# Where GpSimd scales the low words of a weight chunk within a period: behind the masks, or ahead of the clamp

## The chip, the cores and the metric

One core of one Trainium2 chip. The time is that of the device for one execution, in microseconds (us), as the median over several runs. The profile and the trace are of one execution each. The engines are TensorE (PE in the profile; PEld is its weight loads), VectorE (DVE), ScalarE (ACT), GpSimd (POOL) and SyncE (SP), which here issues DMAs.

## What is computed

Attention with a threshold, and behind it a feed-forward block with a squared ReLU:

```python
scores = scale * np.matmul(q, k.transpose(0, 1, 3, 2))      # 8 x 8 heads, 576 x 576, head_dim 64
thresh = np.max(scores, axis=-1, keepdims=True) - tau
scores = np.where(scores >= thresh, scores, -1000000000.0)
attn = np.exp(scores - np.max(scores, axis=-1, keepdims=True))
attn = attn / (np.sum(attn, axis=-1, keepdims=True) + 1e-09)
x = np.matmul(attn, v)                                       # -> 4608 x 512
h = np.maximum(x @ w_in, 0.0)                                # w_in 512 x 2048
return (h * h @ w_out).astype(np.float32)                    # w_out 2048 x 512
```

q, k and v are float32. The two weights are float64: the kernel receives them as 64-bit words and makes float32 of them itself, with integer operations on the two 32-bit halves (the low word and the high word of each number).

## The kernel before

**Stages.** The attention runs first, to about 500 us of the span. Then come the hidden layer and the output layer, both as matrix products with fewer multiplications (seven products of sub-blocks in place of eight, used twice), whose sums and differences VectorE and GpSimd make. The weights are converted from float64 while the attention runs, and are used after it.

**Periods.** The attention works on units of 128 rows of two heads. A period p handles units A = 2p and B = 2p+1. The order in which a period's instructions are issued is written out by hand as a list of step names; each step issues its instructions to its engine, and every engine works through its own in that order. There are two lists: PLAIN, and CONVERTING for the periods in which a chunk of a weight is converted. There are 32 chunks, chunk m starting in period m+2, so that the CONVERTING list is used in periods 2 to 34 (`starts` and `converts`).

**The steps of a period that matter here.** On VectorE: `topA0` to `topB1` (L452) read the scores out of PSUM and take the row maxima; `inv` (L477) takes the reciprocal of the sums of the previous period's units; `maskA1` to `maskB1` (L467) apply the threshold and sum the rows. On ScalarE: `powA0` to `powB1` (L462) are the exponentials, and `eU`, `eV`, `eW`, `x` move results out of PSUM. On GpSimd: `leastA` and `leastB` (L459) make the thresholds from the maxima; `over` (L474) adds 1e-9 to the previous period's sums, which `inv` reads; `xm` (L669) multiplies the previous outcome by the reciprocals. On PE: `SA`, `SB` (L434) are the scores, `U`, `V`, `W` (L380, and L515 for the reciprocals) transpose the weights of the attention, `PV` (L532) multiplies them with the values, `T` (L398) turns later queries and keys.

**The conversion of a chunk** of 128 x 512 numbers goes through six steps over two periods. `fetch` (L191) loads it two periods ahead. In its own period p: `c1` (L205, ScalarE) takes the absolute value of the high words, `c2` (L212, GpSimd) scales the low words in place, `c3` (L219, GpSimd) clamps what c1 made. In the next period: `c4` (L227, VectorE) shifts it, `c5` (L235, VectorE) merges it into the high words, `c6` (L245, GpSimd) adds the low words. So `c2` needs the loaded chunk alone, and only `c6`, a period later, needs what it makes:

```python
nc.gpsimd.tensor_scalar(out=lo, in0=lo.bitcast(U32), scalar1=2.0**-29, scalar2=None, op0=ALU.mult)   # c2, L212
...
nc.gpsimd.tensor_tensor(out=a, in0=hi, in1=lo, op=ALU.add)                                           # c6, L245
```

In CONVERTING periods GpSimd's own order is thus: c3, leastA, over, leastB, c2, c6 (of the chunk before), xm; VectorE's is topA0, topA1, topB0, topB1, c4, inv, maskA1, maskA0, maskB0, c5, maskB1.

Of the kernel before, what the change touches and what calls it, by code (L numbers as in the profile page):

```python
# [48 lines left out]
def kernel(  # L49
# [438 lines left out]
    for g in range(2, 2 * len(pairs)):  # L488
        two, x = divmod(g - 4, 4)
# [99 lines left out]
    def begun(n):  # L589
# [5 lines left out]
        maskB1  # L595
    """.split()
    CONVERTING = """
        fetch SA U eU T SB topA0 s1 c1 topA1 topB0 c3 V PV leastA over powA0 topB1
        powA1 powB0 c4 eT inv x maskA1 maskA0 W leastB maskB0 c5 eV c2 powB1 c6 eW maskB1 xm
    """.split()  # L600

    BEGIN_WITH = {
# [740 lines left out]
```

## Time and profile before

| what | value |
|---|---|
| median of 3 runs | 1300.32 us (1298.04 to 1300.54) |
| span of the profiled execution | 1298.2 us |
| PE busy | 1276.4 us (98%) |
| VectorE busy | 1007.0 us (78%) |
| ScalarE busy | 845.5 us (65%) |
| GpSimd busy | 926.8 us (71%) |
| L212 on GpSimd | 32 times, 65.1 us, first at 26.7 us, last at 246.9 us |
| L245 on GpSimd | 32 times, 47.4 us |
| L219 on GpSimd | 32 times, 19.6 us |
| L459, L474, L669 on GpSimd | 65.9, 17.0, 23.9 us |

The profile gives for each instruction its start, its duration and, where its engine stood idle before it, how long and what ended the wait. The shares are averages over three very different stages; what happens to the conversion is read from the stretch that holds L212, and in it from the order of the instructions in time. Matmuls are pipelined and their ends are modelled, so that PE's share says little of how near it is to its peak.

### The profile page before, as it was taken

What the parts mean: (1) busy time and instruction counts of PE and PEld (TensorE: products, weight loads), DVE (VectorE), ACT (ScalarE), POOL (GpSimd) and SP (SyncE); (2) the same over time, 40 slices, a digit from 0 to 9 for tenths busy, and PEclk for the clock granted to TensorE, in tenths of its full rate; (3) what the DMA queues carried; (4) which work ended last, traced back from release to release, by engine and by line L of the source; (5) the groups of instructions that cost most, each with busy time, mean ns of one, the idle gap of its engine ahead of it and who ended that gap; (6) DMA issues with size and microseconds to landing.
All of it is one profiled execution on the core that took longest, in us unless ns stands there. A gap on an engine that the chain in (4) does not pass through costs nothing.

```text
span 1298.2 us, 45819 instructions
## 1 busy us (share of the span) xinstructions
PE 1276.4 (98%) x18287; PEld 1117.7 (86%) x18287; DVE 1007.0 (78%) x2423; ACT 845.5 (65%) x1498; POOL 926.8 (71%) x1031
## 2 busy tenths in 40 slices
PE   8999999999999999999999999999999999999998
PEld 5777777677777778988888888999999999999998
DVE  6999999999999996886887878867646654665463
ACT  6999999888998984666765856675523432343240
POOL 2787878755555321888897989858787767777775
PEclk8999999999999999999999999999999999999999
DMA  5665566544333312667768768589554224522411
GB/s 143 163 160 154 153 192 180 149 103 110 85 79 80 92 34 64 191 183 218 212 186 226 218 175 235 162 304 391 195 159 164 83 86 159 163 80 88 160 34 34
DMA packets 291413, 196.20 MB, mean 151 GB/s; under 512 B 100096, under 2 KB 252160, under 8 KB 291200
## 3 DMA queue, kind: packets, MB, share of 16 engines
q1 hardware_dynamic: 289888, 192.87, 51.5%
q8 instruction: 144, 2.36, 0.8%
q14 instruction: 69, 0.57, 0.2%
q10 hardware_dynamic: 1312, 0.41, 0.1%
HBM read 120.85 MB, written 72.35 MB: 149 GB/s over the span
## 4 chain that ended last, share of the span: by engine, by line
PE 86%; ACT 5%; DVE 4%; DMA 3%; issue 2%; POOL 0%; SPq 0%; ACTq 0%; DVEq 0%; POOLq 0%
PE po L1077 28%; PE ph L935 16%; PE sc L532 11%; PE sc L434 10%; PE ph L942 10%; PE pt L380 6%; DVE arena L452 2%; PE sc L515 2%; PE sc L398 2%; ACT arena L462 1%; ACT arena L523 1%; DMA g<-arena 1%; PE sc L380 1%; DVE arena L125 1%; DMA wall<-w 1%
## 5 line engine op out<-in xcount | busy, mean ns | idle before, releaser
L125 POOL TENSOR_TENSOR arena<-arena 128x512 f32<-128x512 f32 (+1 forms) x314 | 378.1, 1222 | 147.0 <-DVE arena L125 119.3
L1077 PE MATMUL po<-wall,arena 128*128 128x128 f32 x3528 | 395.0, 275 | 1.9 <-ACT arena L752 1.4
L1077 PEld LDWEIGHTS po<-wall,arena 128*128 128x128 f32 x3528 | 394.4, 192 | 2.5 <-ACT arena L752 1.8
L125 DVE TENSOR_TENSOR arena<-ph,arena 128x512 f32<-128x512 f32 x378 | 255.1, 689 | 79.9 <-PE ph L935 31.5
L122 POOL TENSOR_TENSOR arena<-arena 128x128 f32<-128x128 f32 (+1 forms) x322 | 265.4, 825 | 23.0 <-DMA arena<-w 6.6
L935 PE MATMUL ph<-arena,wall 128*128 128x256 f32 x1176 | 256.6, 380 | 1.8 <-DVE arena L125 1.4
L935 PEld LDWEIGHTS ph<-arena,wall 128*128 128x128 f32 x1176 | 222.2, 190 | 35.9 <-DVE arena L125 5.4
L125 DVE TENSOR_TENSOR arena<-po,arena 128x128 f32<-128x128 f32 x378 | 108.2, 290 | 167.7 <-PE po L1077 163.4
L467 DVE SCALAR_TENSOR_TENSOR arena<-arena 128x576 f32<-128x576 f32 x288 | 235.7, 855 | 0.9 <-ACT arena L462 0.9
L791 ACT COPY c<-arena 128x512 f32<-128x512 f32 (+1 forms) x295 | 169.0, 578 | 71.8 <-DVE arena L122 35.8
L452 DVE TENSOR_SCALAR_CACHE_REDUCE arena<-sc 128x576 f32<-128x576 f32 x288 | 205.1, 748 | 10.9 <-ACT arena L523 4.3
L462 ACT ACTIVATE arena<-arena 128x576 f32<-128x576 f32 x288 | 208.7, 773 | 7.4 <-DVE arena L452 4.2
L532 PEld LDWEIGHTS sc<-arena 64*64 64x64 f32 x5760 | 159.2, 133 | 36.5 <-DVE arena L452 19.8
L532 PE MATMUL sc<-arena 64*64 64x128 f32 (+1 forms) x5760 | 180.5, 262 | 2.9 <-DVE arena L452 1.3
L434 PE MATMUL sc<-arena 64*64 64x64 f32 (+1 forms) x2304 | 176.2, 415 | 3.8 <-ACT arena L403 2.4
L523 ACT COPY arena<-pt 128x1024 f32<-128x1024 f32 x144 | 146.4, 1016 | 27.9 <-PE pt L380 26.5
L122 DVE TENSOR_TENSOR arena<-arena,c 128x512 f32<-128x512 f32 x235 | 154.4, 666 | 11.0 <-ACT c L791 7.6
L752 ACT COPY arena<-po 128x128 f32<-128x128 f32 x63 | 16.6, 264 | 186.4 <-PE po L1077 183.7
L942 PE MATMUL ph<-arena,wall 128*128 128x128 f32 x1176 | 132.0, 275 | 0.7 <-DVE arena L659 0.7
L942 PEld LDWEIGHTS ph<-arena,wall 128*128 128x128 f32 x1176 | 131.6, 192 | 1.1 <-issue 0.8
L380 PEld LDWEIGHTS pt<-ident,arena 64*128 64x128 f32 x2304 | 83.5, 139 | 40.0 <-ACT arena L523 30.1
L434 PEld LDWEIGHTS sc<-arena 64*64 64x64 f32 x2304 | 74.0, 134 | 42.2 <-issue 14.1
(54 smaller groups left out, 1079.7 us busy)
## 6 DMA issues: line engine op xcount, KB each, us to landing
arena<-g SPq DMA_DIRECT2D x144, 256.0 KB, 4.4
g<-arena SPq DMA_DIRECT2D x192, 128.0 KB, 2.9
w<-arena SPq DMA_DIRECT2D x60, 256.0 KB, 2.8
wall<-w SPq DMA_DIRECT2D x49, 256.0 KB, 5.2
g<-arena SPq DMA_DIRECT2D x48, 256.0 KB, 3.8
arena<-w SPq DMA_DIRECT2D x44, 256.0 KB, 3.3
arena<-in_v_dram SPq DMA_DIRECT2D x32, 288.0 KB, 3.8
out_dram<-arena SPq DMA_DIRECT2D x70, 128.0 KB, 2.2
```

What stands on the lines that cost most here:

```text
L122: e.tensor_tensor(out=out, in0=x, in1=y, op=ALU.subtract)
L125: e.tensor_tensor(out=out, in0=x, in1=y, op=ALU.add)
L380: made = nc.tensor.transpose(pt[:, r, ts(slot, HALF)], of[rows, :], ident[rows, rows])
L434: made = nc.tensor.matmul(sc[at, ds(to, count)], lhs, kT[rows, ds(at_k, count)], start=True, stop=True)
L452: made = nc.vector.tensor_scalar(out=s[:, j, :], in0=sc[:, ds(at, S)], scalar1=1.0, scalar2=None, op0=ALU.mult, op1=ALU.min, accum_out=nmx ...
L462: nc.scalar.activation(out=w[:, :, j, :], in_=of(j), func=AF.Exp, bias=nmx[:, j : j + 1], scale=-1.0)
L467: nc.vector.scalar_tensor_tensor(out=w[:, :, j, :], in0=of(j), scalar=thr[:, j : j + 1], in1=w[:, :, j, :], op0=ALU.is_le, op1=ALU.mult, a ...
L532: made = nc.tensor.matmul(sc[ds(u * D, D), ds(5 * j * BANK + row, count)], loaded_v[i][rows, (c - (u != j)) % CH, :], wT[m][rows, ds(weigh ...
L791: nc.scalar.copy(c, y)
L935: nc.tensor.matmul(to[:, 2 * j : 2 * j + 2, :], W_IN[m, k][:, ts(2 * h + j, P)], part_x(steps, k, m), start=(not more and j == 0), stop=Tr ...
L942: nc.tensor.matmul(to[:, j, :], W_IN[m, k][:, ts(j, P)], x, start=(not more and j == 0), stop=True, skip_group_check=True,)
L1077: nc.tensor.matmul(to, g[:, j, :], w[:, j, :], start=(not more and j == 0), stop=(j == 3), skip_group_check=True)
```

## The change

One name moves within one list. The step `c2` stands ahead of `c3`, and no longer behind `eV`:

```diff
     CONVERTING = """
-        fetch SA U eU T SB topA0 s1 c1 topA1 topB0 c3 V PV leastA over powA0 topB1
-        powA1 powB0 c4 eT inv x maskA1 maskA0 W leastB maskB0 c5 eV c2 powB1 c6 eW maskB1 xm
+        fetch SA U eU T SB topA0 s1 c1 topA1 topB0 c2 c3 V PV leastA over powA0 topB1
+        powA1 powB0 c4 eT inv x maskA1 maskA0 W leastB maskB0 c5 eV powB1 c6 eW maskB1 xm
     """.split()
```

GpSimd's order in these periods becomes c2, c3, leastA, over, leastB, c6 (of the chunk before), xm. The order on the other engines and of the DMAs stays as it was, and so do all instructions themselves. The list for the other periods is not touched.

## The prediction

> **What bounds the kernel now.** First the busy time of the engines by stretch, to see which engine is full where the diff acts. The scaling of the low words (L212) is found 32 times, from 26.7 to 246.9 us of the span, so the stretch to look at is about 33 to 255 us. Columns: length, then busy us of PE, PEld, DVE, ACT, POOL, then granted clock, DMA share, GB/s.
>
> ```profile
> core 0: us, PE busy (x) PEld busy (x) DVE busy (x) ACT busy (x) POOL busy (x), PEclk, DMA share, GB/s
> 100.00:140.00 40.00, 39.38 (x961) 29.17 (x958) 40.00 (x111) 38.55 (x70) 32.57 (x42) 1.00 0.59 152
> 33.00:255.00 222.00, 217.95 (x5390) 163.51 (x5386) 221.39 (x594) 213.55 (x385) 177.23 (x217) 1.00 0.62 165
> ```
>
> VectorE is busy without a gap; GpSimd has 18% left over. The page's 98% for PE is no bound here, since ends of matmuls are modelled. The timeline of one period, VectorE and GpSimd alone, shows why. Columns: start, duration, engine, line.
>
> ```profile
> 110.33 0.23 POOL L474 TENSOR_SCALAR arena<-arena 128x4 f32<-128x4 f32 x1
> 110.81 0.17 DVE L477 RECIPROCAL arena<-arena 128x4 f32<-128x4 f32 x1
> 110.89 0.79 DVE L467 SCALAR_TENSOR_TENSOR arena<-arena 128x576 f32<-128x576 f32 x1
> 111.13 2.05 POOL L212 TENSOR_SCALAR arena<-arena 128x512 int32<-128x512 uint32 x1
> 111.61 1.23 DVE L467 SCALAR_TENSOR_TENSOR arena<-arena 128x576 f32<-128x576 f32 x1
> ...
> 112.77 0.81 DVE L467 SCALAR_TENSOR_TENSOR arena<-arena 128x576 f32<-128x576 f32 x1
> 113.50 0.69 DVE L235 SCALAR_TENSOR_TENSOR arena<-arena 128x512 int32<-128x512 int32 x1
> 114.11 0.81 DVE L467 SCALAR_TENSOR_TENSOR arena<-arena 128x576 f32<-128x576 f32 x1
> 114.34 1.48 POOL L245 TENSOR_TENSOR wall<-arena 128x512 int32<-128x512 int32 x1 [1.17 <-DVE arena L235]
> ...
> 115.78 0.73 POOL L669 TENSOR_TENSOR arena<-arena 128x256 f32<-128x256 f32 x1
> 116.47 0.61 POOL L219 TENSOR_SCALAR arena<-arena 128x512 f32<-128x512 f32 x1
> 117.07 0.30 POOL L459 TENSOR_SCALAR arena<-arena,tau_p 128x2 f32<-128x2 f32 x1
> 117.42 0.23 POOL L474 TENSOR_SCALAR arena<-arena 128x4 f32<-128x4 f32 x1
> 117.56 0.42 DVE L227 TENSOR_SCALAR arena<-arena 128x512 int32<-128x512 int32 x1
> 117.89 0.17 DVE L477 RECIPROCAL arena<-arena 128x4 f32<-128x4 f32 x1
> ```
>
> Three things are to be seen. The period, reciprocal to reciprocal, is 117.89 - 110.81 = 7.08 us. GpSimd idles 1.17 us, but behind the scaling, waiting for the merge L235. And two engines form a ring: "over" (L474) must end before the reciprocal (L477), which heads VectorE's masks (L467) and the merge; the merge releases GpSimd's add (L245), then come the normalisation (L669), the clamp (L219), a threshold (L459) and the next "over". Now the ring nearly closes: over ends at 117.65, the reciprocal starts at 117.89. One period shows what happens when the clamp comes late (its operand was late by 1.01 us):
>
> ```profile
> 230.96 0.62 POOL L219 TENSOR_SCALAR arena<-arena 128x512 f32<-128x512 f32 x1 [1.01 <-ACT arena L205]
> 231.02 0.84 DVE L227 TENSOR_SCALAR arena<-arena 128x512 int32<-128x512 int32 x1
> ...
> 232.08 0.23 POOL L474 TENSOR_SCALAR arena<-arena 128x4 f32<-128x4 f32 x1
> 232.34 0.18 DVE L477 RECIPROCAL arena<-arena 128x4 f32<-128x4 f32 x1 [0.49 <-POOL arena L474]
> ```
>
> VectorE stood still for 0.49 us, and the reciprocal started 0.03 us after over ended (232.31). So the spare time of this ring is 117.89 - 117.65 - 0.03 = 0.21 us a period.
>
> **The change, part by part.** Nothing is added or removed: 32 scalings change their place in GpSimd's order, from behind leastB to ahead of the clamp of the same period. No DMA and no other engine's instruction moves. The moved instruction waits only for the load of its chunk, which is issued two periods earlier (14 us, against a median of 4.8 us to landing), so it brings no new wait of its own. What it is moved past are the clamp, leastA, over and leastB: all four now queue behind it, and behind over stand the reciprocal, the four masks and the merge on VectorE.
>
> What goes: the scaling ran beside the masks, and one mask each period took 1.23 us where its neighbours take 0.81; start to start 111.61 to 112.77 is 1.16 against 0.73, so 0.43 us. In its new place the scaling lies beside L452, which reads PSUM; the clamp lies beside L452 now at its plain 0.61 us, so I take the stretch to vanish. Were VectorE still the bound, its period would be 7.08 - 0.43 = 6.65 us.
>
> What comes: the ring, start to start from the rows above. Over's end to reciprocal 0.03; to the first mask 0.08; masks 0.72, 0.73 (without the stretch), 0.73; merge to add 0.84; add 1.44; normalisation 0.69; then the scaling, D, with 0.08 before the next instruction (26.70 + 1.97 to the following L669 at 28.75); clamp 0.60; leastA 0.35; over 0.23. Sum: 6.44 + 0.08 + D = 6.52 + D. The same sum for the kernel before, with the stretch and without the scaling, is 6.87, 0.21 under 7.08 as seen. The 1.17 us of idle time does not help: it stands ahead of the add, and the scaling is now behind it.
>
> D is the open price, since every scaling so far ran beside masks. It starts 0.48 us ahead of the end of one mask (111.61). A small L459 beside a mask shows what such a start means: it took 0.90 us from 232.41 and ended at 233.31, 0.16 us after the next mask began at 233.15, where it takes 0.29 alone; so about 0.13 us of it runs before it is held. The scaling ran 2.05 - 0.48 = 1.57 us past 111.61, and with 0.13 ahead of that D = 1.70. Bounds: 2.13 if it was never held (the longest of its 32), 0.61 as the row furthest away (the clamp, same shape). I take 1.70, by its own row. The ring is then 6.52 + 1.70 = 8.22 us, which is above 6.65, so GpSimd's part of the ring decides and VectorE idles 8.22 - 6.65 = 1.6 us ahead of each reciprocal.
>
> A rule of the Trainium skill bears on the stretch. Page "SBUF — State Buffer", section "Who interferes with whom": a VectorE instruction with two SBUF inputs contends with a GpSimd instruction that reads SBUF, and the later one is blocked until the first is done. The trace agrees on which rows suffer (masks yes, L452 no) and differs on how long: the mask lost 0.43 us of the scaling's 2.05. By the rule in full the shift L227 would now be caught beside the scaling; that outcome is a rival below.
>
> The sum over the stretch. From the reciprocal of the second period with a scaling (33.08) to that of the last (246.54) are 30 rings, 213.46 us now (30 x 7.08 and 1 us of small delays). The second period's own over ends at 32.27, and its scaling falls into 1.59 us in which GpSimd waited for L205 anyway (the first one into 5.17 us), so the new count starts at 32.30: 32.30 + 30 x 8.22 = 278.9 us. That is 32.4 later than 246.54. The period after the last scaling runs without the stretch, -0.4. Together +32.0 us. What follows (plain periods, then the two layers) has no catching up: it is a chain that starts later. The profiled execution has a span of 1298.2 us, 2.1 under the median of the runs, 1300.3; I carry the difference to the median: 1300.3 + 32.0 = 1332 us. With D = 1.57 (nothing of it runs before it is held) the ring is 8.09 and the sum +28; with D = 2.13 it is 8.65 and +45. So 1328 to 1345 for this case.
>
> ScalarE and PE should not add to that. PE goes from one recip fill (L380 at 111.37) to the next (118.62) in 7.25 us, under 8.22; ScalarE's Abs (L205), which the clamp needs, ends 1.5 us after the merge (115.68 against 114.19), some 4.5 us after over's end, and the clamp starts 7.0 us after it in the new ring.
>
> **The rivals.**
> - Slower still, by a collision: L227 (start 117.56) falls beside the scaling or the clamp, as at 231.02, where it took 0.84 instead of 0.42, and this time the clamp is the one that is held. Costs up to L227's 0.34 a ring: 8.56, 32.30 + 256.8 - 246.54 - 0.4 = +42, 1342 us. For it: L227 would start some 6.3 us after over's end, the scaling some 5.3. Against it: the one row shows L227 held, not GpSimd, and VectorE has time to wait. The rule quoted above gives this case.
> - Slower, but less, because the scaling is shorter undisturbed: with 1.28 us, the float add of the same shape (L125), the ring is 7.80 and the sum +19, 1320 us. Against it: 1.57 us of the scaling lie behind the mask that held it.
> - No change: D as short as the clamp, 0.61, gives a ring of 7.13 and 32.30 + 213.9 - 246.54 - 0.4 = -0.7, 1300 us. The point from which the ring decides is D = 0.55.
> - Faster: the scaling's cover holds, over is in time, and only the stretch goes: 32 x 0.43 = 13.8 us, 1287 us. This needs 6.52 + D under 6.65, D under 0.13, or an over that does not gate the reciprocal; the 0.49 us at 232 us speaks against the latter. The same for a change that does nothing: GpSimd's order does move, all 32 times.
>
> **How the numbers follow.** Forecast 0.75 (1328 to 1345), collision 0.10, shorter scaling 0.08, no change 0.03, faster 0.04. A measurement of this kernel can tell about 0.2% (2.6 us) from nothing; by these cases faster is 0.04, the same 0.03, slower 0.93. The range takes in the forecast's bounds, the collision and part of the shorter scaling: 1321 to 1347. The time is the forecast's, 1332.
>
> **What would show it.** Right: between 40 and 280 us a period of about 8.2 us; the wait of L477 for L474 about 30 times, 1.2 to 1.6 us each; L212 between L669 and L219 with about 1.7 us; no mask above 0.85 us; POOL L245 still waiting for L235, 2 to 2.7 us; last scaling near 275 us and everything after it later by one constant. Wrong: VectorE still gapless there with a period near 6.65 (over is no gate), L212 far under 1.5 us (D), L227 or L219 stretched (collision), or a wait of L477 that is made up for after 280 us.

## The result, and the profile after

The changed kernel takes 1335.35 us (1333.61 to 1335.68, 4 runs) against 1299.18 us (1297.27 to 1300.54, 4 runs) in the same comparison: 1.0278 times as long, 95% interval 1.0263 to 1.0293, or 36 us more. The profiled execution has a span of 1333.9 us, 35.7 more than the one before.

First the busy time by stretch, now to 285 us, since the last scaling has moved to 279.5 us (the columns are those of the same view before).

```profile
33.00:285.00 252.00, 214.13 (x5240) 149.09 (x5229) 220.09 (x575) 209.68 (x373) 175.56 (x210) 1.00 0.54 142
```

VectorE is busy for 220 us, as before (221), but now in 252 us and no longer in 222. What it waits for is in the view of its waits for this stretch (who waited, for whom, us in total, times, longest):

```profile
DVE arena L477 <- POOL arena L474: 31.9, 30, 1.1
```

30 waits of 1.06 us, all ahead of the reciprocal, all for "over". The timeline of one period, VectorE and GpSimd alone, shows what "over" is late for:

```profile
110.20 1.48 POOL L245 TENSOR_TENSOR wall<-arena 128x512 int32<-128x512 int32 x1 [2.17 <-DVE arena L235]
...
111.64 0.72 POOL L669 TENSOR_TENSOR arena<-arena 128x256 f32<-128x256 f32 x1
112.45 1.63 POOL L212 TENSOR_SCALAR arena<-arena 128x512 int32<-128x512 uint32 x1
113.42 0.94 DVE L227 TENSOR_SCALAR arena<-arena 128x512 int32<-128x512 int32 x1
114.16 0.66 POOL L219 TENSOR_SCALAR arena<-arena 128x512 f32<-128x512 f32 x1
114.80 0.29 POOL L459 TENSOR_SCALAR arena<-arena,tau_p 128x2 f32<-128x2 f32 x1
115.16 0.23 POOL L474 TENSOR_SCALAR arena<-arena 128x4 f32<-128x4 f32 x1
115.42 0.18 DVE L477 RECIPROCAL arena<-arena 128x4 f32<-128x4 f32 x1 [1.06 <-POOL arena L474]
...
116.23 0.81 DVE L467 SCALAR_TENSOR_TENSOR arena<-arena 128x576 f32<-128x576 f32 x1
```

From the add to "over" GpSimd works with no gap above 0.09 us, and its own idle time, 2.17 us, stands ahead of the add, where it waits for the merge. No mask takes more than 0.82 us: the long one of 1.23 is gone. The shift L227 has become longer instead, 0.94 us where it took 0.42; more on that below. The period from reciprocal to reciprocal is 8.35 us in the mean of 30 rings ((282.44 - 31.89) / 30), against 7.12 before ((246.54 - 33.08) / 30). At the first reciprocal behind the conversions the changed kernel is 35.5 us later (289.12 against 253.59), and at the end 35.7: what follows starts later and takes as long as before.

### The profile page after: what moved, and what is told of

It reads as the page before. It is cut to its first block, busy times and chain, and to the rows that moved or that the text cites. A ratio compares the mean times of both kernels' runs of the same rounds, so it can differ in the third digit from the quotient of the medians.

```text
span 1333.9 us, 45819 instructions
## 1 busy us (share of the span) xinstructions
PE 1277.9 (96%) x18287; PEld 1107.2 (83%) x18287; DVE 1012.1 (76%) x2423; ACT 846.8 (63%) x1498; POOL 929.1 (70%) x1031
## 4 chain that ended last, share of the span: by engine, by line
PE 69%; ACT 5%; DVE 3%; POOL 3%; DMA 3%; issue 2%; SPq 0%; POOLq 0%; ACTq 0%; DVEq 0%
PE po L1077 26%; PE ph L935 17%; PE ph L942 9%; PE sc L532 5%; PE sc L434 5%; PE pt L380 3%; ACT arena L462 1%; ACT arena L523 1%; PE sc L398 1%; DVE arena L452 1%; POOL arena L212 1%; PE sc L515 1%; DVE arena L125 1%; DMA arena<-g 1%; POOL arena L245 1%
## 5 line engine op out<-in xcount | busy, mean ns | idle before, releaser
L935 PEld LDWEIGHTS ph<-arena,wall 128*128 128x128 f32 x1176 | 222.3, 190 | 35.7 <-DVE arena L125 5.7
L467 DVE SCALAR_TENSOR_TENSOR arena<-arena 128x576 f32<-128x576 f32 x288 | 223.1, 812 | 1.1 <-ACT arena L462 1.1
L532 PEld LDWEIGHTS sc<-arena 64*64 64x64 f32 x5760 | 159.2, 133 | 46.6 <-DVE arena L452 33.0
L434 PE MATMUL sc<-arena 64*64 64x64 f32 (+1 forms) x2304 | 172.3, 413 | 2.6 <-ACT arena L403 2.3
L459 POOL TENSOR_SCALAR arena<-arena,tau_p 128x2 f32<-128x2 f32 x144 | 79.7, 554 | 42.3 <-DVE arena L452 37.2
```

The source lines that it names most:

```text
L434: made = nc.tensor.matmul(sc[at, ds(to, count)], lhs, kT[rows, ds(at_k, count)], start=True, stop=True)
L467: nc.vector.scalar_tensor_tensor(out=w[:, :, j, :], in0=of(j), scalar=thr[:, j : j + 1], in1=w[:, :, j, :], op0=ALU.is_le, op1=ALU.mult, a ...
L532: made = nc.tensor.matmul(sc[ds(u * D, D), ds(5 * j * BANK + row, count)], loaded_v[i][rows, (c - (u != j)) % CH, :], wT[m][rows, ds(weigh ...
L935: nc.tensor.matmul(to[:, 2 * j : 2 * j + 2, :], W_IN[m, k][:, ts(2 * h + j, P)], part_x(steps, k, m), start=(not more and j == 0), stop=Tr ...
```

## The experiments

Nine more kernels were run. They test the theory of a ring (over, reciprocal, masks, merge, add, normalisation, whatever GpSimd does next, over) against the rival that the scaling costs time by holding up what VectorE does beside it.

**A known amount ahead of the clamp, with the scaling in its old place.**

```diff
+    def extra(m):
+        if m is not None:
+            for _ in range(1):                        # 3 in the second run
+                nc.gpsimd.tensor_scalar(
+                    out=spare[:, :], in0=ident[:, 0:2], scalar1=tau_p[:, :], scalar2=None, op0=ALU.add
+                )
...
-        fetch SA U eU T SB topA0 s1 c1 topA1 topB0 c3 V PV leastA over powA0 topB1
+        fetch SA U eU T SB topA0 s1 c1 topA1 topB0 extra c3 V PV leastA over powA0 topB1
```

> The kernel before, scaling in its old place, and one small GpSimd instruction (128x2, like L459, about 0.29 us and 0.06 us to the next) ahead of the clamp in each period with a chunk; its result is not used. Ring theory (everything GpSimd does between the add L245 and over L474 counts one to one, once the spare 0.21 us is used up): ring 6.87 + 0.35 = 7.22 us, a period of about 7.22 instead of 7.07; the first ring still has 0.8 us to spare, so +2.5 to +4 us, about 1302.5 against 1299.2. Rival, the price comes from the scaling's neighbours at the shared SBUF port and not from the order of the queue: a 128x2 instruction reads next to nothing, so the period stays 7.07 and the time 1299.

> As the run with one small instruction, with three of them (about 1.05 us) ahead of the clamp. Ring theory: 6.87 + 1.05 = 7.92 us a period, VectorE waits for over about 0.85 us before each reciprocal, +24 us, 1323 us. Rival (port, not queue): no small instruction holds up VectorE, 1299 to 1301 us.

Measured: 1.0055 times the kernel before (1.0043 to 1.0068), 1306.2 us, period 7.33 us, with one; 1.0230 (1.0214 to 1.0245), 1328.5 us, period 8.08, with three, and 30 waits of the reciprocal for "over" of 0.48 us (this kernel is eight lines longer, so that they are L485 and L482 here):

```profile
DVE arena L485 <- POOL arena L482: 14.5, 30, 0.5
```

One instruction occupies GpSimd's queue for 0.26 us to the next start, three for 1.03; the second step adds 0.77 us to the queue and 0.75 us to the period. So work ahead of "over" counts one to one, although it reads next to nothing. Both periods are 0.11 to 0.16 us longer than expected (and the times 4 to 6 us): with one instruction the shift L227 falls beside "over" (0.37 us instead of 0.23), with three beside the clamp and leastA (0.46 instead of 0.29), which the expectation left out.

**No scaling at all** (list of the changed kernel without `c2`).

```diff
-        nc.gpsimd.tensor_tensor(out=a, in0=hi, in1=lo, op=ALU.add)
+        nc.gpsimd.tensor_tensor(out=a, in0=hi, in1=hi, op=ALU.subtract)
```

> No scaling at all (the step c2 is left out; so that all numbers stay finite the add L245 takes the high words minus themselves, and the weights come out as zeros). Ring theory: without the scaling the ring is 6.44 us and VectorE, without the stretched mask, needs 6.65: the period is 6.65, VectorE has no gap, -13 us, 1286 us. If the mask's 0.43 us came from something else than the scaling: period 7.07, 1299. If the ring is longer than I take it to be, the period lies between 6.65 and 7.07 and VectorE waits for over.

Measured: 0.9977 (0.9966 to 0.9987), 1296.6 us, and not 1286. Most periods are 6.67 to 6.75 us, as expected, and VectorE does not wait for over; but nine of 31 take some 7.7 us, which is most of the 10 us that were missed. The timeline shows both kinds, mask and add side by side (start, duration):

```profile
48.34 1.70 DVE L467 SCALAR_TENSOR_TENSOR arena<-arena 128x576 f32<-128x576 f32 x1
48.38 1.04 POOL L245 TENSOR_TENSOR wall<-arena 128x512 int32<-128x512 int32 x1 [2.81 <-DVE arena L235]
...
55.94 0.82 DVE L467 SCALAR_TENSOR_TENSOR arena<-arena 128x576 f32<-128x576 f32 x1
56.06 1.60 POOL L245 TENSOR_TENSOR wall<-arena 128x512 int32<-128x512 int32 x1 [2.81 <-DVE arena L235]
```

In eight of the nine the add starts 0.04 us or less behind the mask, takes 1.04 us itself, and the mask takes 1.57 to 1.70; where it starts 0.09 us or more behind, the mask takes 0.82 at most and the add 1.54 to 1.63. Nothing lies between. (In the ninth, from 205.86 us, no mask is long: there a mask waits 0.95 us for an exponential of ScalarE.) In the kernels before and after the add starts 0.19 to 0.26 us behind the mask, and the mask goes first. To test this, the add was made a little later:

```diff
+        nc.gpsimd.tensor_scalar(
+            out=spare[:, :], in0=hi[:, 0:2].bitcast(FP32), scalar1=tau_p[:, :], scalar2=None, op0=ALU.add
+        )
         nc.gpsimd.tensor_tensor(out=a, in0=hi, in1=hi, op=ALU.subtract)
```

> As the run without the scaling (weights come out as zeros), and a 128x2 instruction on GpSimd ahead of each add L245 that reads two merged words, so that it waits for the merge L235 and the add starts about 0.3 us later, when the mask next to it has been running for a while. Theory: in the run without the scaling the add began within 0.04 us of the mask in about a third of the periods, took the shared SBUF port first and held the mask for 0.88 us; started later it never does. Then no mask takes more than 0.85 us, and all periods are at VectorE's 6.67 or at the ring's 6.44 + 0.3 = 6.75: 1286 to 1290 us. Rival (the 1.02 us of these periods come from a late exponential on ScalarE, the port only follows): a third of the periods stay at 7.7, 1297 us.

Measured: 0.9963 (0.9945 to 0.9980), 1293.4 us, above the expected 1290. No mask takes over 0.9 us any more (eight did without the small instruction), and the run of periods of 7.7 us is gone, so for the eight the order of add and mask was the cause and not ScalarE. Two long periods are left, of 8.0 and 7.8 us, in which VectorE waits once 1.2 us for PE and once 1.1 us for "over", behind a late clamp. The usual period is 6.88, not 6.75: the small instruction itself waits for the mask (0.72 us instead of 0.29), and "over" is again beside the shift (0.38). VectorE's pace of 6.65 us is thus seen in most periods of the run without the small instruction, but in no whole execution.

**The scaling behind over, ahead of leastB.**

```diff
-        fetch SA U eU T SB topA0 s1 c1 topA1 topB0 c3 V PV leastA over powA0 topB1
+        fetch SA U eU T SB topA0 s1 c1 topA1 topB0 c3 V PV leastA over c2 powA0 topB1
```

(with `c2` taken out of the second line of the list)

> The scaling behind over and ahead of leastB: of the four instructions that it was moved past in the change, only leastB stays behind it. Ring theory: over and leastA are on time, but leastB ends at 2.1 to 3.1 us after over, and the mask maskB0 waits for it, which would start at 1.6 (2.0 with a stretched mask): a period of 7.0 to 8.0, say 7.5, and the wait now stands ahead of a mask L467 on L459, not ahead of L477: 1299 to 1327, say 1312 us. Rival (only over gates VectorE): 7.07 as before, 1299 us. Rival (the scaling costs by its neighbours): beside the masks as in the kernel before, 7.07.

Measured: 1.0046 (1.0033 to 1.0059), 1305.1 us, period 7.31. Timeline of one period, GpSimd and VectorE alone:

```profile
111.97 1.73 POOL L212 TENSOR_SCALAR arena<-arena 128x512 int32<-128x512 uint32 x1
...
112.23 1.13 DVE L467 SCALAR_TENSOR_TENSOR arena<-arena 128x576 f32<-128x576 f32 x1
...
113.80 0.47 POOL L459 TENSOR_SCALAR arena<-arena,tau_p 128x2 f32<-128x2 f32 x1
...
114.30 0.82 DVE L467 SCALAR_TENSOR_TENSOR arena<-arena 128x576 f32<-128x576 f32 x1 [0.19 <-POOL arena L459]
```

The wait has moved to where the theory put it: ahead of a mask, for the threshold leastB, 30 times 0.19 us. It is shorter than expected, since leastB slips in between two masks and takes 0.47 us only. The first mask is held for 0.34 us (1.13 against the 0.79 that the first mask of a period takes otherwise), somewhat less than the mask beside the scaling before.

**Scaling and clamp both behind leastB.**

```diff
-        powA1 powB0 c4 eT inv x maskA1 maskA0 W leastB maskB0 c5 eV c2 powB1 c6 eW maskB1 xm
+        powA1 powB0 c4 eT inv x maskA1 maskA0 W leastB c2 c3 maskB0 c5 eV powB1 c6 eW maskB1 xm
```

> Scaling and clamp together behind leastB, beside the masks: neither stands ahead of over any more. Ring theory: the ring is 0.6 us shorter than in the kernel before, VectorE decides with its 7.07 us and up to 0.43 us that the clamp takes from a second mask or the merge: 7.07 to 7.5 us, 1299 to 1312 us, no wait of L477 for L474. Rival (two large GpSimd instructions in a row hold VectorE until both are done): over 8 us, 1328 us or more.

Measured: 1.0085 (1.0067 to 1.0103), 1309.4 us, period 7.48, and no wait of L477. VectorE is the bound: a mask of 1.23 us beside the scaling and a merge L235 of 1.10 (0.69 otherwise) beside the clamp (0.79 us): 6.65 + 0.43 + 0.41 = 7.49.

**The merge ahead of the masks**, which cuts the ring with the scaling left where the change put it.

```diff
-        powA1 powB0 c4 eT inv x maskA1 maskA0 W leastB maskB0 c5 eV powB1 c6 eW maskB1 xm
+        powA1 powB0 c4 c5 eT inv x maskA1 maskA0 W leastB maskB0 eV powB1 c6 eW maskB1 xm
```

> The changed kernel, and besides VectorE's merge c5 (L235) ahead of the reciprocal and the masks, right behind the shift c4. The add L245 then no longer waits for the masks, and the ring is cut, with the scaling still ahead of the clamp. Ring theory: GpSimd alone needs about 6.2 us a period; VectorE decides with 6.65 us and what the add and the normalisation, now beside masks, take from it (0.43 for 512 words read, 0.85 for the add's two inputs): 7.1 to 7.9 us, 1299 to 1324, say 1312. VectorE has no gap ahead of the reciprocal. Rival (the scaling beside L227 and the clamp is what costs): the period stays at 8.35, 1335 us.

Measured: 1.0331 (1.0315 to 1.0346), 1340.6 us, period 8.42, far above the expected 1299 to 1324. By the time alone the rival would seem right; the timeline says otherwise:

```profile
109.66 1.54 POOL L245 TENSOR_TENSOR wall<-arena 128x512 int32<-128x512 int32 x1 [0.72 <-DVE arena L477]
...
110.23 1.59 DVE L467 SCALAR_TENSOR_TENSOR arena<-arena 128x576 f32<-128x576 f32 x1
111.17 1.24 POOL L669 TENSOR_TENSOR arena<-arena 128x256 f32<-128x256 f32 x1
...
111.75 1.27 DVE L467 SCALAR_TENSOR_TENSOR arena<-arena 128x576 f32<-128x576 f32 x1
112.50 1.98 POOL L212 TENSOR_SCALAR arena<-arena 128x512 int32<-128x512 uint32 x1
...
112.96 1.19 DVE L467 SCALAR_TENSOR_TENSOR arena<-arena 128x576 f32<-128x576 f32 x1
```

VectorE has no wait in this stretch, L227 is at its plain 0.42 us, and GpSimd now idles 1.9 us a period: the ring is cut, and the collision of L227 is gone too. But the add, the normalisation and the scaling each lie beside a mask, and the masks lose 0.78, 0.46 and 0.38 us: 6.65 + 1.62 = 8.27 of 8.42 (the shift before the merge takes 0.12 more of it: 116.79 to 117.25 start to start, 0.34 otherwise). The expectation counted 0.85 for the add and 0.43 for the normalisation, and forgot that the scaling then falls beside the last mask.

**Half a scaling, in the new place and in the old one.**

```diff
-            nc.gpsimd.tensor_scalar(out=lo, in0=lo.bitcast(U32), scalar1=2.0**-29, scalar2=None, op0=ALU.mult)
+            nc.gpsimd.tensor_scalar(out=lo[:, 0 : WC // 2], in0=lo[:, 0 : WC // 2].bitcast(U32), scalar1=2.0**-29, scalar2=None, op0=ALU.mult)
...
-        nc.gpsimd.tensor_tensor(out=a, in0=hi, in1=lo, op=ALU.add)
+        nc.gpsimd.tensor_tensor(out=two_of(a), in0=two_of(hi), in1=twice, op=ALU.add)
```

(`two_of` views the 512 columns as two halves, and `twice` reads the scaled half two times.)

> The changed kernel with a scaling of half the size: it scales 256 of the 512 low words of each row, and the add takes this half twice, so the other half of the low words is left out. Ring theory: the scaling takes (1.63 - 0.13) / 2 + 0.13 = 0.88 us, the ring 8.35 - 0.75 = 7.60, perhaps 7.55 because L227 no longer meets it; 1311 to 1313 us. If most of the scaling were a fixed cost: 8.0 or more, 1324. Rival (the price is that L227 and the clamp collide with the scaling): with the collision gone the period falls to the 7.07 or 6.65 of VectorE, 1299 or below.

> The kernel before with a scaling of half the size (the other half of the low words is left out, the add takes the scaled half twice). It lies beside the masks. If the mask is held while the scaling reads its input, one word after another: held 0.21 instead of 0.43 us, period 6.86, -6.5 us, 1293 us. If it is held once for a fixed time: period 7.07, 1299 us. If the mask waits until the scaling has ended, it would have lost 1.57 us with the whole scaling, which it did not.

Measured in the new place: 1.0178 (1.0159 to 1.0198), 1320.6 us, period 7.87, not 7.60. The scaling takes 0.92 us (0.88 expected), but the add that takes the half twice needs 1.70 instead of 1.46; 8.35 - 1.63 + 0.92 + 0.24 = 7.88, so the ring accounts for it. The shift L227 is hardly caught any more (0.47 us), and the 30 waits of 1.06 us for "over" are still there (`DVE arena L480 <- POOL arena L477: 31.9, 30, 1.1`; this kernel is three lines longer). So the collision is not what VectorE waits for. In the old place: 1.0000 (0.9989 to 1.0011), 1297.7 us and not 1293, period 7.08. By the period alone a hold of a fixed time would seem right; the mask says otherwise. The mask is held for 0.20 us (1.01 against 0.81), as expected, but the time did not fall: with the longer add (1.73) and "over" beside the shift (0.40) the ring is 6.44 + 0.20 + 0.25 + 0.17 = 7.06. This run settles the size of the hold and, by a side effect of the edit, nothing on the time that a shorter hold would save.

No version with the whole computation was faster than the kernel before.

## Why the prediction was right

**What bounds the stretch.** VectorE without a gap, and a ring with 0.21 us to spare: held. With one small instruction the ring reckons to 6.87 + 0.26 (queue) + 0.15 (over beside the shift) = 7.28, and the period was 7.33: there was no more to spare than the 0.21 us.

**What goes.** The 0.43 us of the long mask left with the scaling, as predicted; without any scaling the undisturbed periods are 6.67 us (6.65 predicted).

**What comes.** The ring was put at 6.52 + 1.70 = 8.22 us and is 8.35. Two terms were mis-sized against each other. D is 1.63 and not 1.70, so the idea that a scaling is held by the mask that it meets, and then runs 1.57 us, came within 0.07 of it. The 0.08 us that GpSimd needs between the scaling and its neighbour was counted once; it stands on both sides (111.64 + 0.72 to 112.45 leaves 0.09, where the clamp used to start 0.04 ahead of the normalisation's end), 0.12 us more. The clamp took 0.64 us to the next start instead of 0.60, and the masks' starts lie 0.02 further apart in all. By rows: 0.03 + 0.09 + 0.72 + 0.74 + 0.74 + 0.83 + 1.44 + 0.81 + 1.71 + 0.64 + 0.36 + 0.23 = 8.34.

**The sum.** 30 rings cost 250.55 - 213.46 = 37.1 us where 246.6 - 213.5 = 33.1 had been reckoned. The reciprocal of the second period came at 31.89 instead of the assumed 32.30; it lies between 30.8 and 33.6 in the profiles of the nine experiments, and I give no cause for its place here. The last period gave back 0.37 us (0.4 predicted). That is 37.1 - 1.2 - 0.4 = 35.5 us, against 32.0. That 1332 us lies so near to the measured 1335 is partly luck: D, too long, hid about a third of what the other rows of the ring lacked, the early reciprocal took 0.4 us off, and the kernel before was 1.1 us faster here than the median from which the forecast set out.

**The signs.** The wait for "over" was forecast at 1.2 to 1.6 us and is 1.06, since the held L227 fills 0.52 us of what would have been idle time on VectorE. A stretched L227 had been named as a sign of being wrong; the others came as forecast, the last scaling 4.5 us later than the 275 named. The prediction also calls D = 0.55 the point from which the ring decides; by its own numbers that is D = 0.13 (6.65 - 6.52), and at 0.55 the change would merely cost nothing.

**The rivals.** The collision of L227 did happen: it took 0.94 us instead of 0.42, in all 30 periods that hold both it and a scaling. The part of the rival that costs time did not: L227 was the one held, VectorE had 1.06 us left to wait after it, and the clamp lost 0.05 us, not 0.34. The prediction quotes the rule for instructions with two SBUF inputs; L227 has one, so that the rule as quoted there does not give this case. The Trainium skill, "SBUF — State Buffer", section "Who interferes with whom", has the second of two instructions wait until the first is done. For L227 beside the scaling that is nearly what the trace shows (held until 0.14 us ahead of the scaling's end); for a mask it is not (0.43 of 2.05 us, and 0.20 with half the words). A shorter scaling, no change and a faster kernel fell with D = 1.63 and the 30 waits.

**ScalarE and PE** add nothing: VectorE's waits in the stretch are those for "over" alone.

## What to carry to other kernels

Idle time of an engine is worth something only at its place in the order: GpSimd had 1.2 us free in every period, behind the scaling, and moving the scaling away from it put 1.7 us on a ring that had 0.2 to spare. Before an independent piece of work is moved ahead in an engine's queue, follow the first result that leaves that queue after it, here a 128x4 instruction of 0.23 us that heads all of VectorE's masks. And the old slot, beside VectorE's masks, which looks bad (0.4 us lost), was cheaper here than every other place that was tried.

## What the runs showed of the hardware

- What a mask loses beside a GpSimd instruction went with the words per partition that this reads, and not with its duration: 0.20 us for 256 (scaling of 1.40 us), 0.34 to 0.43 for 512 (scaling of 1.73 to 2.05 us), 0.46 for 2 x 256 (normalisation of 1.24 us), 0.78 to 0.88 for 2 x 512 (add of 1.54 and 1.04 us). The merge lost 0.41 us beside the clamp (512 words, 0.79 us).
- Whether the mask or the add goes first turned on 0.05 us (0.04 or 0.09 us between their starts), and the whole period on that: 6.7 or 7.7 us in the run without the scaling.
- GpSimd's durations contain the wait for VectorE: the add of the run without the scaling takes 1.04 us when it goes first and 1.54 to 1.63 behind a mask, the scaling 1.63 away from the masks and 2.05 beside them, a 128x2 threshold 0.29 and 0.90.
- The shift L227, from SBUF to SBUF with one input, is held almost until the GpSimd instruction beside it has ended: to 0.14 us ahead of the scaling's end (0.52 us lost), and with three small instructions to 0.14 us ahead of the clamp's (0.42 lost). A mask is let go much earlier, 1.15 us ahead of the scaling's end in the kernel before. Why the two differ, no run tested.
